# Moving the decay loads of units 8 to 11 from SyncE's DMA queue to GpSimd's in a gated linear attention and expert kernel

## The chip, the cores and the metric

The kernel runs on one core of a Trainium2 chip. The metric is the device time of one execution in microseconds (us); each kernel is run several times and the median stands for it. The kernel before took a median of 179.3 us over five runs, from 176.89 to 180.84 us.

## The reference

Two layers follow each other. The first is a gated linear attention with 4 batches, 8 heads, 768 tokens and a head size of 48. The second is a dense layer with a squared ReLU, from 384 features to 2048 and back, over all 3072 tokens.

```
for t in range(S):
    state = alpha[:, :, t, :, None] * state + np.einsum('bhd,bhe->bhde', k[:, :, t], v[:, :, t])
    y[:, :, t] = np.einsum('bhd,bhde->bhe', q[:, :, t], state)
...
h = x @ w_in
r = np.maximum(h, 0.0)
g = r * r
return (g @ w_out).astype(np.float32)
```

`alpha` is the decay: a number between 0.8 and 1 for every token, head and feature.

## The kernel before, in words

**Units.** The 3072 tokens are cut into 12 units of 256 tokens. Unit g is one block of one batch; units 0 to 3 are the first blocks of the four batches, 4 to 7 the second, 8 to 11 the last. For each unit four inputs are loaded (`load`, line 508): the decays `a`, then `k`, `q` and `v`, 384 KB each, as runs of 384 bytes, into one of four `RAW` buffers.

**Stages of a unit.** The front (`front`, `decays_by_pair`) multiplies the decays of a pair of tokens (`prd`, VectorE, line 615), takes logarithms (`lab` and `la`, ScalarE, lines 618 and 657), sums them along the tokens with a matmul (line 624), takes exponentials (`ek`, `eq`), and multiplies `k` and `q` by them (`qks`, lines 691 and 686). From unit 3 on, two DMA transposes on SyncE's queue turn the result (`kqt`, line 702). Scores follow on TensorE (line 880), a mask on VectorE (`pm`, line 891), the output and the state (lines 772, 783, 751), a copy out of PSUM (`xbf`, line 911) and, for units 4 to 10, one more DMA transpose on SyncE's queue (`xt`, line 932). The dense layer (`moe`) then works through the 2048 hidden features: the first product (line 983) into two PSUM banks in turn, a ReLU that empties each bank (`rr`, ScalarE line 991 or VectorE line 993), a square (`gt`, lines 1001 and 1005), the second product (line 1019), a copy (`osb`) and a store on SyncE's queue (line 1029). The dense work of one unit lies between the attention work of the next.

**What sets the order.** Every instruction is handed to a planner (`Program.add`) with an estimated cost, a priority and the instructions that it depends on. `Program.schedule` plays the program through with these estimates and writes down a fixed order for each engine; some instructions may go to one of two engines, and the planner picks. On the chip every engine runs its list strictly in that order and waits at the head of it, with semaphores placed by `Program.place`. So an estimate that changes can change the order on every engine. For DMAs the planner uses the issue cost (600 ns on SyncE, 930 on GpSimd), a delay to the first byte (`DMA_FIRST`), the transfer time alone (`lag`), and, where several queues have work, shares in proportion to the numbers of `PACKET`, found by the first prefix that matches the operation's name.

**Who gates the loads.** From unit 4 on each load of unit g waits until `q` of unit g-1 has landed (`AFTER`), and from unit 5 on also for a step of unit g-1 (`BEHIND`): its logarithm for `a`, its product for `k`, its first transpose for `q` and `v`. SyncE's queue carries all loads but those of unit 2, which go with the weights through GpSimd's queue, and it carries all transposes and stores as well.

Of the kernel before, what the change touches and what calls it, by code (L numbers as in the profile page):

```python
# [33 lines left out]
class Program:  # L34
# [3 lines left out]
    HOP = 35  # L38
    PE_LATENCY = 170
    DMA_FIRST = {"sp": 1300, "act": 1300, "pool": 2000}  # L40
    PACKET = (("win", 172), ("wout", 490), ("ld", 22), ("tr", 18), ("xt", 18), ("out", 65))
    SBUF_ONLY = ("pr", "bk", "aq", "ekm", "eqm", "sq", "sb", "sd")
    BIAS = {"pool": 300}
    DMA_LAST = 800
# [13 lines left out]
    def add(self, eng, fn, cost, prio, reads=(), writes=(), name="", dma=None, lag=0, after=(), mode=("F", "F"),  # L58
            alts=None):

        reads, writes = ([h for k in keys for h in ((k + (0,), k + (1,)) if len(k) == self.HALVED.get(k[0]) else (k,))]
                         for keys in (reads, writes))
        choices = {eng: (fn, cost)}
        if alts:
            choices.update(alts)
        op = Op(choices, prio, name)
        op.idx = len(self.ops)
        op.lag = lag
        op.mode = mode
        if dma is not None:  # L70
            if dma not in self.dma_sems:
                self.dma_sems[dma] = self.nc.alloc_semaphore("d_" + dma)
                self.dma_count[dma] = 0
            self.dma_count[dma] += 1
            op.sem = (dma, self.dma_count[dma])
        for o in after:
            op.deps[o] = True
        for k in reads:
            w = self.writer.get(k)
            if w is not None:  # L80
                op.deps[w] = True
            if k[0] == "ps":
                for r in self.readers.get(k, ()):
                    op.deps.setdefault(r, False)
        for k in writes:
            w = self.writer.get(k)
            if w is not None:
                op.deps[w] = True
            for r in self.readers.get(k, ()):
                if r is not op:  # L90
                    op.deps.setdefault(r, False)
        for k in reads:
            self.readers.setdefault(k, []).append(op)
        for k in writes:
            self.writer[k] = op
            self.readers[k] = []
        op.deps.pop(op, None)
        self.ops.append(op)
        return op

    def schedule(self):
# [18 lines left out]
        def rates():  # L120
            took = {r: next(t for n, t in self.PACKET if q[0].name.startswith(n)) for r, q in rings.items() if q}
            return {r: t / sum(took.values()) for r, t in took.items()}
# [200 lines left out]
def pe_ns(count, cols, at_once=1):  # L323
    return count * max(cols / 2.4 + 2.5, 25) / at_once
# [6 lines left out]
def dve_ns(n, rate=1.0):  # L331
    return 150 + n / 0.96 / rate
# [6 lines left out]
def bass_gla_recurrent__then__act_relu_squared_kernel(  # L339
# [18 lines left out]
    G = B * NST  # L358
# [4 lines left out]
    ATTN = {1: 13665, 2: 25972, 3: 40856, 4: 50288}  # L363
    DENSE = {0: 21894, 1: 33515, 2: 47958, 3: 58770, 11: 158500}
    POOL_LOADS = {2: "akqv"}
    RATIO = 4
    NRAW, NQKS, NKQT, NPM, NV, NXT, NGT, NRR, NOSB = 4, 3, 3, 2, 4, 4, 2, 4, 4
    WS = 2
# [48 lines left out]
    add = pr.add  # L417
# [17 lines left out]
    for i in range(2):  # L435
        add("dve", fill(LAF[i][:, :, :, D:64].rearrange("p j h d -> p (j h) d"), 0.0), 250, -1e6 - 10,
            writes=[("laf", i)])
        add("dve", fill(LAB[i][:, :, D:64], 0.0), 150, -1e6 + 20, writes=[("lab", i)])
    for i in range(NQKS):
        add("dve", fill(QKS[i][:, :, :, :, D:64].rearrange("p a j h d -> p (a j h) d"), 0.0), 500, -1e6 + 10,  # L440
            writes=[("qks", i, 0), ("qks", i, 1)])
# [7 lines left out]
    for part in (OWN[0:64, 0:H:2], OWN[64:128, 1:H:2]):  # L449
# [3 lines left out]
        writes=[("ident",)])  # L453
# [29 lines left out]
    load_op = {}  # L483
# [4 lines left out]
    def named(x):  # L488
        return next(o for o in pr.ops if o.name == x)

    BEHIND = {"a": "ln", "k": "ekm", "q": "tr0_", "v": "tr0_"}

    def load(g):
        b, i = units[g]
        t0 = i * T
        p0 = g * P
        r, la, qs, kt, pm, vb, x2 = (g % n for n in (NRAW, 2, NQKS, NKQT, NPM, NV, 2))
        first, last = i == 0, i == NST - 1
        sr, sw = 2 * b + i % 2, 2 * b + (i + 1) % 2

        for j, t, nm in ((0, alpha, "a"), (1, k, "k"), (2, q, "q"), (3, v, "v")):
            src = t[b, :, t0:t0 + T, :].rearrange("h (p j) d -> p h (j d)", j=2)
            dst, key = RAW[r][:, j], ("raw", r, j)
            ring, cost, gate = "sp", 600, AFTER.get((g, nm), AFTER.get(g))
            if nm in POOL_LOADS.get(g, ""):
                ring, cost = "pool", 930
            dst = dst.rearrange("p h j d -> p h (j d)")
            load_op[g, nm] = add(ring, lambda e, dst=dst, src=src: e.dma_start(dst, src), cost, (L_PRIO[g] + j if ring == "sp" else W_PRIO[2] + 10 * g + j),  # L508
                writes=[key], name=f"ld{nm}{g}", dma=f"{nm}{r}{ring}", lag=1230,
                after=([load_op[gate]] if gate else []) + ([named(f"{BEHIND[nm]}{g - 1}")] if g >= 5 else []))  # L510

    def front_by_heads(g, p0):

# [96 lines left out]
    def decays_by_pair(g, p0, r, la, last):  # L610
# [11 lines left out]
        def m1(incl):  # L622
            def run(pe):
                ins = pe.matmul(psW[:, 0:HD], (LINC if incl else LSTR)[:], LAB[la][:, :, 0:D])  # L624
                if incl and not last:
                    for p in range(NPR):
                        ins = pe.matmul(psW[:, HD + 2 * p:HD + 2 * p + 2],  # L627
                                        LAB[la][:, 2 * p:2 * p + 2, :].rearrange("p h d -> p (h d)"), ONES2[:],
                                        start=(p == 0), stop=True, skip_group_check=True)
                return ins  # L630
            return run
# [7 lines left out]
        if not last:  # L639
# [5 lines left out]
                          dve_ns(HD))})  # L645
        if g < RATIO:
            add("pe", m1(False), pe_ns(1, HD), p0 + 530, reads=[("lab", la), ("lstr",)], writes=[("ps", "W")],
# [384 lines left out]
    L_PRIO = {g: (g - 4) * P for g in range(G)}  # L1032
    L_PRIO[0], L_PRIO[1] = -9e5, -8e5
    W_PRIO = (-5e5, -4e5, -4.5e5)
    ORDER = ["f0", "k0", "p0", "f1", "y0", "p1", "k1", "y1", "f2", "p2", "k2"]
    for g in range(3, G):
# [3 lines left out]
             ("wout", 1): (2, "k"), 3: ("wout", 0)}  # L1040
    AFTER.update({g: (g - 1, "q") for g in range(4, G)})
    load(0)
    load(1)
    for w in range(WS):
        weight(0, w)
    load(2)
    for w in range(WS):
        weight(1, w)
    for st in ORDER:
        kind, g = st[0], int(st[1:])  # L1050
# [44 lines left out]
```

## Time and profile before

| | us |
|---|---|
| median of five runs | 179.3 |
| the profiled execution, its own time | 178.37 |
| span of that execution | 176.6 |
| TensorE busy in the span | 168.3 |
| VectorE / ScalarE busy | 120.0 / 120.1 |
| GpSimd busy | 15.2 |

The span is the time from the first to the last instruction that the profiler saw. The granted TensorE clock was 1.000. TensorE is busy in 95% of the span, and GpSimd in 9%, nearly all of it in the first 40 us. Of the DMA queues, SyncE's (q1) moved 28.12 MB in 73968 packets and GpSimd's (q0) 4.72 MB in 1536 packets.

From the trace come the times of the loads of the decays. An issue is where the queue's instruction starts; the landing is counted from it.

| unit | decay load issued at, us | us to landing |
|---|---|---|
| 7 | 72.64 | 4.6 |
| 8 | 86.99 | 3.3 |
| 9 | 99.12 | 3.4 |
| 10 | 111.24 | 3.6 |
| 11 | 124.53 | 4.3 |

### The profile page before, as it was taken

What the parts mean: (1) busy time and instruction counts of PE and PEld (TensorE: products, weight loads), DVE (VectorE), ACT (ScalarE), POOL (GpSimd) and SP (SyncE); (2) the same over time, 40 slices, a digit from 0 to 9 for tenths busy, and PEclk for the clock granted to TensorE, in tenths of its full rate; (3) what the DMA queues carried; (4) which work ended last, traced back from release to release, by engine and by line L of the source; (5) the groups of instructions that cost most, each with busy time, mean ns of one, the idle gap of its engine ahead of it and who ended that gap; (6) DMA issues with size and microseconds to landing.
All of it is one profiled execution on the core that took longest, in us unless ns stands there. A gap on an engine that the chain in (4) does not pass through costs nothing.

```text
span 176.6 us, 5120 instructions
## 1 busy us (share of the span) xinstructions
PE 168.3 (95%) x2241; PEld 130.4 (74%) x2241; DVE 120.0 (68%) x198; ACT 120.1 (68%) x215; POOL 15.2 (9%) x24
## 2 busy tenths in 40 slices
PE   7999898999999999999999999996999999999994
PEld 2566797856778777877878788794788697698773
DVE  5597959696949898749589678777759727352230
ACT  4762779677877699659399578496578564475541
POOL 3250740020010003100000000000000000000000
DMA  5999999999999798998599899999797691110112
GB/s 144 324 294 198 279 282 205 231 254 287 214 217 192 199 232 140 261 250 165 157 290 148 229 211 229 253 198 219 196 176 192 150 184 36 45 45 4 45 45 89
DMA packets 75526, 33.16 MB, mean 188 GB/s; under 512 B 70896, under 2 KB 74096, under 8 KB 75504
## 3 DMA queue, kind: packets, MB, share of 16 engines
q1 hardware_dynamic: 73968, 28.12, 69.6%
q0 software_dynamic: 1536, 4.72, 12.1%
q8 instruction: 17, 0.28, 0.6%
q14 instruction: 5, 0.04, 0.1%
HBM read 25.17 MB, written 4.72 MB: 169 GB/s over the span
## 4 chain that ended last, share of the span: by engine, by line
PE 70%; DMA 20%; DVE 3%; SPq 2%; ACT 2%; issue 1%; POOL 1%
PE psWH L983 31%; PE psO L1019 27%; DMA win<-in_moe_w_in_dram 7%; DMA raw<-in_alpha_dram 5%; DMA kqt<-qks 3%; DMA xt<-xbf 3%; DMA raw<-in_q_dram 2%; PE psX L783 2%; SPq L508 2%; PE psX L880 2%; PE psZ L751 2%; PE psX L953 2%; PE psX L772 1%; PE psZ L880 1%; PE psWH L624 1%
## 5 line engine op out<-in xcount | busy, mean ns | idle before, releaser
L983 PE MATMUL psWH<-xt,win 128*128 128x256 bf16 x576 | 74.0, 275 | 3.1 <-DMA xt<-xbf 1.5
L983 PEld LDWEIGHTS psWH<-xt,win 128*128 128x128 bf16 x576 | 64.8, 145 | 8.0 <-DMA xt<-xbf 2.1
L1019 PE MATMUL psO<-wout,gt 128*128 128x384 bf16 x368 | 68.9, 326 | 0.1
L991 ACT ACTIVATE rr<-psWH 128x512 bf16<-128x512 f32 x82 | 48.0, 595 | 22.9 <-PE psWH L983 21.4
L1019 PEld LDWEIGHTS psO<-wout,gt 128*128 128x128 bf16 x368 | 35.1, 98 | 18.3 <-ACT osb L1026 0.3
L1001 DVE TENSOR_TENSOR gt<-rr 128x1024 bf16<-128x1024 bf16 (+1 forms) x40 | 24.0, 602 | 20.4 <-ACT rr L991 20.1
L891 DVE TENSOR_TENSOR pm<-psX,caus 128x1024 bf16<-128x1024 f32 x12 | 14.6, 1218 | 3.9 <-PE psZ L880 3.9
L1005 ACT ACTIVATE gt<-rr 128x512 bf16<-128x512 bf16 (+1 forms) x20 | 16.4, 821 | 0.5
L891 DVE TENSOR_TENSOR pm<-psZ,caus 128x1024 bf16<-128x1024 f32 x12 | 14.6, 1216 | 0.8 <-PE psZ L880 0.8
L686 DVE TENSOR_TENSOR qks<-raw,eq 128x384 bf16<-128x384 f32 x18 | 9.3, 554 | 8.6 <-DMA raw<-in_q_dram 7.0
L1026 ACT ACTIVATE osb<-psO 128x384 f32<-128x384 f32 x19 | 9.3, 492 | 6.3 <-PE psO L1019 5.7
L682 ACT ACTIVATE vbf<-raw 128x768 bf16<-128x768 f32 x10 | 8.4, 842 | 6.8 <-DMA raw<-in_v_dram 6.6
L1063 PE MATMUL psO<-zero 128*128 128x512 bf16 (+1 forms) x35 | 9.7, 412 | 1.3 <-DVE zero L429 1.3
L911 ACT ACTIVATE xbf<-psX 128x768 bf16<-128x768 f32 x11 | 8.9, 805 | 3.0 <-PE psX L772 1.9
L691 DVE TENSOR_TENSOR qks<-raw,ek 128x768 bf16<-128x768 f32 x11 | 10.4, 949 | 0.0
L993 DVE TENSOR_SCALAR rr<-psWH 128x512 bf16<-128x512 f32 x14 | 9.6, 687 | 0.9 <-PE psWH L983 0.3
L657 ACT ACTIVATE la<-raw 128x384 f32<-128x384 f32 x8 | 4.2, 522 | 5.9 <-DMA raw<-in_alpha_dram 5.9
L1063 PEld LDWEIGHTS psO<-zero 128*128 128x128 bf16 x35 | 3.4, 108 | 4.9 <-issue 1.9
L615 DVE TENSOR_TENSOR prd<-raw 128x384 f32<-128x384 f32 x7 | 3.9, 559 | 4.1 <-DMA raw<-in_alpha_dram 4.1
L644 DVE TENSOR_TENSOR ek<-ek,raw 128x384 f32<-128x384 f32 x10 | 5.5, 555 | 1.1 <-ACT ek L635 1.1
L635 ACT ACTIVATE ek<-psWH 128x384 f32<-128x384 f32 x10 | 4.9, 495 | 1.4 <-PE psWH L627 1.4
L751 PE MATMUL psZ<-vbf,qks 64*128 64x96 bf16 x144 | 5.6, 202 | 0.0
(114 smaller groups left out, 159.3 us busy)
## 6 DMA issues: line engine op xcount, KB each, us to landing
out_dram<-osb SPq DMA_DIRECT2D x23, 192.0 KB, 3.1
raw<-in_alpha_dram SPq DMA_DIRECT2D x11, 384.0 KB, 4.3
raw<-in_k_dram SPq DMA_DIRECT2D x11, 384.0 KB, 4.6
raw<-in_q_dram SPq DMA_DIRECT2D x11, 384.0 KB, 4.5
raw<-in_v_dram SPq DMA_DIRECT2D x11, 384.0 KB, 4.9
win<-in_moe_w_in_dram POOLq DMA_DIRECT2D x2, 768.0 KB, 10.0
wout<-in_moe_w_out_dram POOLq DMA_DIRECT2D x2, 768.0 KB, 8.9
raw<-in_alpha_dram POOLq DMA_DIRECT2D x1, 384.0 KB, 5.8
```

Of the source, the lines that this page charges most:

```text
L686: add("dve", lambda e, j=j, dst=dst: e.tensor_tensor(dst, RAW[r][:, 2, :, j, :].rearrange("p (n x) d -> p n x d", x=2), EQ[la][:, j].rearr ...
L691: add("dve", lambda e, a=a, E=E: e.tensor_tensor(QKS[qs][:, a, :, :, 0:D], RAW[r][:, 1 + a].rearrange("p h j d -> p j h d"), E[la][:].rear ...
L751: ins = pe.matmul(banks[c][:, p * 96:p * 96 + 96], QKS[qs][h0:h0 + 64, 0, j, 2 * p:2 * p + 2, :].rearrange("p h d -> p (h d)"), VBF[vb][h0 ...
L891: add("dve", lambda e, hf=hf, psT=psT: e.tensor_tensor(PM[pm][:, hf].rearrange("p r n j t -> p (r n) (j t)"), psT[:, :, :].rearrange("p r ...
L983: ins = pe.matmul(psH[hb][:, i * T:(i + 1) * T], WIN[:, kk, hidden(fj)], mov, start=(kk == 0), stop=(kk == KT - 1))
L991: add("act", lambda e, hb=hb, rr=rr: e.activation(rr, psH[hb], AF.Relu), act_ns(512), pu + 600, reads=[("ps", "H", hb)], writes=[("rr", rb ...
L993: alts={"dve": (lambda e, hb=hb, rr=rr: e.tensor_scalar(rr, psH[hb], 0.0, None, ALU.max), dve_ns(512))})
L1001: add("dve", lambda e, dst=dst, sq=sq: e.tensor_tensor(dst, sq, sq, ALU.mult), 148 + k * 267, pu + 1200, reads=[("rr", rb, h) for h in ran ...
L1005: "act": (lambda e, dst=dst, sq=sq: e.activation(dst, sq, AF.Square), act_ns(k * 512))})
L1019: ins = pe.matmul(psS, GT[gt][:, fj, j, :], WOUT[:, fj, :], start=(fj == 0), stop=(fj == FT - 1))
L1026: add("act", lambda e, ob=ob, psS=psS: e.activation(OSB[ob][:], psS, AF.Copy), act_ns(DM), ps_ + 700, reads=[keyS], writes=[("osb", ob)], ...
L1063: pr.fill(lambda n: lambda pe: pe.matmul(psO[:, 0:n], ZERO[:, 0:128], ZERO[:, 0:n], skip_group_check=True), ((512, 216, 420), (256, 109, 2 ...
```

## The change

The decay loads of units 8, 9, 10 and 11 are issued by GpSimd instead of SyncE. The gates stay as they are, and the other loads stay on their queues. In the planner, GpSimd's loads get names that begin with `ldp`, and with that a number of their own in `PACKET`; their transfer time becomes 1080 ns instead of 1230; this holds for the four loads of unit 2 as well, which went through GpSimd's queue before. For units 8 to 11 the planner's priority is that of the other loads of the unit. The semaphores' names lose the queue's name and gain a `p`.

```diff
-    PACKET = (("win", 172), ("wout", 490), ("ld", 22), ("tr", 18), ("xt", 18), ("out", 65))
+    PACKET = (("win", 172), ("wout", 490), ("ldp", 175), ("ld", 22), ("tr", 18), ("xt", 18), ("out", 65))
...
     POOL_LOADS = {2: "akqv"}
+    POOL_FROM, POOL_WHICH = 8, "a"
+    POOL_LOADS.update({g: POOL_WHICH for g in range(POOL_FROM, G)})
...
             if nm in POOL_LOADS.get(g, ""):
                 ring, cost = "pool", 930
+                nm = "p" + nm
             dst = dst.rearrange("p h j d -> p h (j d)")
-            load_op[g, nm] = add(ring, lambda e, dst=dst, src=src: e.dma_start(dst, src), cost, (L_PRIO[g] + j if ring == "sp" else W_PRIO[2] + 10 * g + j),
-                writes=[key], name=f"ld{nm}{g}", dma=f"{nm}{r}{ring}", lag=1230,
-                after=([load_op[gate]] if gate else []) + ([named(f"{BEHIND[nm]}{g - 1}")] if g >= 5 else []))
+            load_op[g, nm[-1]] = add(ring, lambda e, dst=dst, src=src: e.dma_start(dst, src), cost, (L_PRIO[g] + j if ring == "sp" else W_PRIO[2] + 10 * g + j if g < 3 else L_PRIO[g] + j),
+                writes=[key], name=f"ld{nm}{g}", dma=f"{nm}{r}", lag=1080 if ring == "pool" else 1230,
+                after=([load_op[gate]] if gate else []) + ([named(f"{BEHIND[nm[-1]]}{g - 1}")] if g >= 5 else []))
```

## The prediction

> **What bounds the kernel now.** I began with the page's busy table and groups, then cut the span into stretches of one unit, from one output on TensorE to the next, around the four moved loads:
>
> ```profile
> 89.70:102.20 12.50, 12.50 (x181) 9.82 (x183) 10.28 (x17) 9.38 (x18) 0.00 (x0) 1.00 1.00 223
> 102.20:114.70 12.50, 12.50 (x176) 10.03 (x176) 9.95 (x16) 9.23 (x16) 0.00 (x0) 1.00 0.98 226
> 114.70:128.90 14.20, 12.71 (x175) 9.93 (x176) 9.70 (x16) 9.33 (x17) 0.00 (x0) 1.00 0.91 212
> 128.90:141.40 12.50, 12.50 (x175) 10.02 (x177) 9.69 (x15) 9.43 (x16) 0.00 (x0) 1.00 0.88 164
> ```
>
> The columns are length, then busy us (and instructions) of TensorE, its weight loads, VectorE, ScalarE and GpSimd, then clock, share of DMA time and GB/s. TensorE is busy in 12.50 of 12.50 us. GpSimd does nothing, and the DMA engines are occupied nearly all the time. Only the third stretch has a hole. The chain of waits shows it:
>
> ```profile
> 118.02 0.69 PE psWH L983 x7
> 118.71 4.70 DMA xt<-xbf
> 123.46 0.88 PE psWH L983 x6
> ```
>
> The first dense product waited for its transposed input; the same transpose landed in 2.7 to 2.9 us in the six other units. TensorE lost about 1.5 us here, the largest loss in this half. So the end is set by TensorE, and the moved loads matter only where they make it wait.
>
> Do they? ScalarE's timeline around the load of unit 8:
>
> ```profile
> 88.77 1.07 ACT L991 ACTIVATE rr<-psWH 128x512 bf16<-128x512 f32 x2
> 90.27 0.52 ACT L657 ACTIVATE la<-raw 128x384 f32<-128x384 f32 x1 [0.43 <-DMA raw<-in_alpha_dram]
> 90.70 0.48 ACT L1026 ACTIVATE osb<-psO 128x384 f32<-128x384 f32 x1
> 91.07 0.51 ACT L618 ACTIVATE lab<-prd 128x384 bf16<-128x384 f32 x1
> 91.48 0.80 ACT L911 ACTIVATE xbf<-psX 128x768 bf16<-128x768 f32 x1
> 92.17 1.08 ACT L991 ACTIVATE rr<-psWH 128x512 bf16<-128x512 f32 x2
> ```
>
> The logarithm stands at the head of ScalarE until the decays land, and behind it queue the output copy, a second logarithm and two ReLUs. TensorE's next first product starts at 92.82 with a wait for one of these ReLUs. In all, between 84 and 140 us ScalarE waits 4.2 us for decays, once per unit. The decays are therefore already the last thing to arrive at ScalarE, though TensorE hides most of it.
>
> The loads were not held up on SyncE's queue. Between 84 and 140 us this queue waits 12.6 us, in four waits, for `q` of the unit before, and issues the decays at once when it lands: `q` of unit 7 was issued at 81.72 and took 5.2, which makes 86.92, and the decays follow at 86.99. The change keeps that gate, so no decay load can start sooner.
>
> **What the skill says.** The page "DMA: Bandwidth & Descriptors" bears on it in three places. "Latency and other measured facts" puts the first byte at some 600 ns for SyncE's queue and 1 us for GpSimd's; the trace shows the issue itself at 0.37 us for SyncE's decay loads and 0.95 for GpSimd's one. "SWDGE vs HWDGE vs iDMA" says that the queues feed different rings of one DMA engine, served in turn by packet, and that GpSimd's packets gather up to 4096 bytes. The trace agrees on sizes: 4.72 MB in 1536 packets is 3.07 KB each, 28.12 MB in 73968 is 380 bytes, a ratio of 8. "Issuing engines are not separate DMA queues" says that spreading loads saves only issue time; no run yet shows it. On starved descriptors the page "SBUF — State Buffer", "SBUF: two separate sides", warns of VectorE blocking GpSimd; the trace has GpSimd's four load issues at 0.95 and 0.89 us beside a VectorE busy for 9.04 of 10 us, so I price that at nothing, at most another issue of 0.9.
>
> **The price of the moved load.** Removed from SyncE: four issues of 0.37 us and four transfers. Added to GpSimd: four waits and four issues of 0.95 us. GpSimd's last work was at 73.88 us, so nothing queues behind the wait; if the new order put arithmetic there, the waiting time would fall on whoever needs it.
>
> Its latency without a queue ahead is not shown. GpSimd's loads of unit 2 stood in line behind weights: 5.8 us for the decays. Their landings come out at 23.3, 24.5, 25.6 and 26.5, so one load's data takes 1.07 us. The first weight piece, issued at 9.31, landed 7.9 later, at 17.2; the second at 22.27, 5.07 after it. Taking these 5.07 as the data of one piece leaves 2.8 us for everything else. My estimate for a decay load is 2.8 + 1.07 = 3.9 us from issue. GpSimd also reacts later: 17.2 to 17.53 and 22.27 to 22.55, about 0.28 us, against 0.07 on SyncE. So from the gate 4.2 us, against 3.4, 3.5, 3.7 and 4.4 before (the landing times plus 0.07). Later by 0.8, 0.7, 0.5 and -0.2 us for units 8 to 11. The bounds: every load as fast as SyncE's, since its larger packets take turns against small ones, hence 0; and the 5.8 of unit 2, hence 5.8 + 0.28 - 3.4 = 2.7 later.
>
> What of it reaches TensorE, with the order unchanged? In unit 8 the ReLU is already waited for, so there is no slack. In unit 9 the first ReLU behind the logarithms ends at about 104.8 and TensorE's next first product starts at 105.22: 0.4. In units 10 and 11 it is 117.2 to 117.70 and 131.4 to 131.90: 0.5 each. Stalls: 0.8, 0.3, 0 and 0, **1.1 us together**. The later work of the front is covered: `qks` for `q` at 99.2 us waits for `q`, not for the decays.
>
> **Relief on SyncE.** The second transpose of a unit is held up while loads drain: the first issues took 2.88, 3.37 and 2.86 us in units 8 to 10 (at 100.26, 112.38 and 125.97) against 1.24 for the quickest. One load less ahead frees up to 1.1 us (one load's data), and the stores and `xt` behind it move up. The `xt` issued at 93.92 lands at 96.7, and TensorE needs it at 96.78, so that is worth something when it is late: at most the hole of 1.5 us. I take 0, since one late landing in seven may be chance. The saved data time, 1.23 (the code's own estimate) less 1.07, is 0.16 us a load, and TensorE covers it.
>
> **The order.** The names and `lag` of unit 2's loads change in the planner, four times 150 ns, and GpSimd's transfers there now take 175 shares beside 22 and 18 of SyncE's. Priorities and due times stay. So the order can move on all engines from about 23 us on, although unit 2's transfers themselves are unchanged. Nothing in the trace prices this. From below: the early idle of TensorE between 20 and 60 us, 1.33 + 0.14 + 0.43 + 0.36 = 2.3 us by its busy times, could shrink, say by 1.5. From above: an extra 0.5 us in each of six or seven units, 3. I take +0.9 because `xt`, the ReLUs and `kqt` arrive within a few tenths of their use, and TensorE has nothing spare to win.
>
> **Sum.** 178.37, the profiled execution's own time, + 1.1 + 0 + 0.9 = 180.4. This execution is 0.9 below the median of 179.3, so the forecast for the median is **181.3 us**, 1.1% above.
>
> **Rivals.** (1) *The late decays decide; slower.* If the landing is later by L in each unit, stalls sum to 4L - 1.4 (slacks 0, 0.4, 0.5, 0.5). With L = 1.5, inside my bounds, that is 4.6, and with 0.9 for the order 178.37 + 0.93 + 5.5 = 184.8. From L of about 1.0 on, the loss passes 2%. For it: two engines wait at their heads for the decays already, and 3 KB packets may hold up transposes beside them. Against: the planner itself expects GpSimd's load later and may put other work first. (2) *The relief decides.* `xt` is never late, the hole of 1.5 closes, decays land as before: 179.3 - 1.5 = 177.8; with a luckier early order down to 175.5. Against: decays would have to be no later, and TensorE's 168.3 busy us stay. (3) *The change doesn't do what it says:* loads move at no cost and only the new order shows, anywhere from -1.5 to +3, about 180.2.
>
> **Chances.** The forecast 0.44, rival 1 0.36, rival 2 0.14, rival 3 0.06. Runs of this kernel spread over 2.2%, so about 2% (3.6 us) is what a measurement can tell from no change. Slower than 182.9: all of rival 1, 0.06 of the forecast and 0.02 of rival 3, 0.44. Faster than 175.7: 0.05 of rival 2 and 0.03 of rival 3, 0.08. Between: 0.48. Both ends of the order's price and a lateness up to 1.8 us give a range of 177.5 to 187.0; the forecast's own is 179.5 to 183.2.
>
> **What would show it.** Right: decay issues on GpSimd near 0.95 us, landing 3.7 to 4.4 later; about 0.3 us from gate to issue; ScalarE's waits for decays in units 8 to 11 above 4.2 us, or the logarithms placed behind other work; unit stretches of 12.5 to 13.3 us. Wrong: landings above 5 us or long waits for ReLUs on TensorE (rival 1); second transposes unblocked and no wait for `xt` (rival 2); differences before 84 us that outweigh those after (the order was mispriced). It would also be wrong if GpSimd had been given arithmetic behind its waits.

## The result, and the profile after

The changed kernel took a median of 178.85 us over 36 runs (176.19 to 181.72), the kernel before 178.22 us over 71 runs (175.48 to 180.95). The ratio is 1.0051, with a 95% interval from 1.0029 to 1.0073: slower by about 0.9 us, where the forecast had been 2.0 us slower. The medians are of all executions, while ratios and intervals, here and below, compare only those within 1.5% of a kernel's fastest. The spread of single runs, 5.5 us, is six times the difference, so the reasons have to be read from places in the trace and not from the total alone.

The profiled execution of the changed kernel took 181.72 us, the longest of its runs, and its TensorE clock fell to 0.90 for one stretch; three further profiles of the same kernel (below) therefore stand beside it. In the changed kernel the lines move: the decay load is line 511, the first dense product 986, the ReLUs 994 (ScalarE) and 996 (VectorE).

From the page of the changed kernel, its DMA queues and two groups of instructions:

```profile
q1 hardware_dynamic: 69808, 26.55, 66.5%
q0 software_dynamic: 1984, 6.29, 15.1%
...
L511 POOL DMA_DIRECT2D raw<-in_alpha_dram x5 | 4.6, 912 | 53.4 <-DMA raw<-in_q_dram 36.1
...
L684 POOL CAST vbf<-raw 128x768 bf16<-128x768 f32 x7 | 6.1, 871 | 29.6 <-DMA raw<-in_v_dram 29.5
```

Four loads of 384 KB have gone from the first queue to the second, in 448 packets more there and 4160 fewer here, and each issue costs GpSimd 0.91 us on average, as predicted. What the prediction had only mentioned as a risk is in the last line: GpSimd now makes seven casts of `v`, one before. The planner gave it those of units 8 to 11, right behind the loads, and those of units 2 and 4. GpSimd's timeline in the changed kernel:

```profile
85.43 0.96 POOL L511 DMA_DIRECT2D raw<-in_alpha_dram  x1 [10.99 <-DMA raw<-in_q_dram]
98.79 0.89 POOL L511 DMA_DIRECT2D raw<-in_alpha_dram  x1 [12.40 <-ACT rr L994]
99.74 0.83 POOL L684 CAST vbf<-raw 128x768 bf16<-128x768 f32 x1
112.80 0.88 POOL L511 DMA_DIRECT2D raw<-in_alpha_dram  x1 [12.23 <-DMA raw<-in_q_dram]
```

The loads of units 8 to 11 landed 5.7, 7.4, 4.8 and 6.0 us after issue; before it had been 3.3, 3.4, 3.6 and 4.3. What the 7.4 did is in VectorE's, ScalarE's and TensorE's timeline of the changed kernel:

```profile
106.22 0.52 ACT L660 ACTIVATE la<-raw 128x384 f32<-128x384 f32 x1 [3.21 <-DMA raw<-in_alpha_dram]
106.22 0.56 DVE L618 TENSOR_TENSOR prd<-raw 128x384 f32<-128x384 f32 x1 [5.47 <-DMA raw<-in_alpha_dram]
106.65 0.79 ACT L914 ACTIVATE xbf<-psX 128x768 bf16<-128x768 f32 x1
106.70 0.55 DVE L849 TENSOR_TENSOR smd<-psZ,sbd 128x384 bf16<-128x384 f32 x1
107.17 0.68 DVE L996 TENSOR_SCALAR rr<-psWH 128x512 bf16<-128x512 f32 x1
...
107.90 1.50 PE L986 MATMUL psWH<-xt,win 128*128 128x256 bf16 x6 [2.26 <-DVE rr L996]
```

Both engines stand at the head of their lists until the decays come, VectorE for 5.47 us. The ReLU that would empty TensorE's PSUM bank is third in VectorE's list, so TensorE waits 2.26 us for a ReLU whose own input had been ready all along. This is the predicted kind of stall, larger than predicted. The wait of 1.5 us for `xt` of the kernel before is absent: in none of the four profiles of the changed kernel does TensorE wait for `xt` more than 0.12 us. Late transposes are not gone, though. The `xt` issued between 130 and 135 us lands 3.8 to 4.6 us after issue in all four, just in time for TensorE.

### The profile page after: what moved, and what is told of

Read it like the earlier page. It is cut to its first block, busy times and chain, and to the rows that moved or that the text cites. A ratio compares the mean times of both kernels' runs of the same rounds, so it can differ in the third digit from the quotient of the medians.

```text
span 180.0 us, 5139 instructions
## 1 busy us (share of the span) xinstructions
PE 171.1 (95%) x2241; PEld 131.4 (73%) x2241; DVE 115.0 (64%) x188; ACT 121.6 (68%) x219; POOL 24.2 (13%) x34
## 4 chain that ended last, share of the span: by engine, by line
PE 44%; DMA 33%; ACT 8%; SPq 6%; DVE 5%; issue 2%; POOL 1%; DVEq 0%
PE psWH L986 19%; PE psO L1022 17%; DMA raw<-in_alpha_dram 16%; DMA raw<-in_q_dram 9%; DMA win<-in_moe_w_in_dram 4%; ACT rr L994 3%; DMA raw<-in_v_dram 3%; SPq L705 2%; SPq L511 2%; PE psX L956 1%; SPq L1032 1%; DVE pm L894 1%; ACT eq L640 1%; DVE rr L996 1%; ACT ek L638 1%
## 5 line engine op out<-in xcount | busy, mean ns | idle before, releaser
L986 PE MATMUL psWH<-xt,win 128*128 128x256 bf16 x576 | 75.5, 278 | 3.4 <-DVE rr L996 2.6
L994 ACT ACTIVATE rr<-psWH 128x512 bf16<-128x512 f32 x88 | 51.8, 595 | 23.5 <-PE psWH L986 22.1
L1004 DVE TENSOR_TENSOR gt<-rr 128x1024 bf16<-128x1024 bf16 (+1 forms) x39 | 23.3, 601 | 23.3 <-ACT rr L994 23.0
L1008 ACT ACTIVATE gt<-rr 128x512 bf16<-128x512 bf16 (+1 forms) x21 | 17.5, 833 | 0.5
L1029 ACT ACTIVATE osb<-psO 128x384 f32<-128x384 f32 x22 | 10.8, 492 | 10.2 <-PE psO L1022 9.6
L511 POOL DMA_DIRECT2D raw<-in_alpha_dram x5 | 4.6, 912 | 53.4 <-DMA raw<-in_q_dram 36.1
L694 DVE TENSOR_TENSOR qks<-raw,ek 128x768 bf16<-128x768 f32 x11 | 11.4, 1034 | 0.0
L684 POOL CAST vbf<-raw 128x768 bf16<-128x768 f32 x7 | 6.1, 871 | 29.6 <-DMA raw<-in_v_dram 29.5
L849 DVE TENSOR_TENSOR smd<-psZ,sbd 128x384 bf16<-128x384 f32 x8 | 4.4, 552 | 4.8 <-PE psX L775 4.8
L996 DVE TENSOR_SCALAR rr<-psWH 128x512 bf16<-128x512 f32 x8 | 5.5, 688 | 0.7 <-PE psWH L986 0.5
```

Source lines behind the costliest of these rows:

```text
L511: load_op[g, nm[-1]] = add(ring, lambda e, dst=dst, src=src: e.dma_start(dst, src), cost, (L_PRIO[g] + j if ring == "sp" else W_PRIO[2] + ...
L694: add("dve", lambda e, a=a, E=E: e.tensor_tensor(QKS[qs][:, a, :, :, 0:D], RAW[r][:, 1 + a].rearrange("p h j d -> p j h d"), E[la][:].rear ...
L986: ins = pe.matmul(psH[hb][:, i * T:(i + 1) * T], WIN[:, kk, hidden(fj)], mov, start=(kk == 0), stop=(kk == KT - 1))
L994: add("act", lambda e, hb=hb, rr=rr: e.activation(rr, psH[hb], AF.Relu), act_ns(512), pu + 600, reads=[("ps", "H", hb)], writes=[("rr", rb ...
L1004: add("dve", lambda e, dst=dst, sq=sq: e.tensor_tensor(dst, sq, sq, ALU.mult), 148 + k * 267, pu + 1200, reads=[("rr", rb, h) for h in ran ...
L1008: "act": (lambda e, dst=dst, sq=sq: e.activation(dst, sq, AF.Square), act_ns(k * 512))})
```

## The experiments

All ratios are to the kernel before, timed in the same session, each with its 95% interval. Several kernels use a helper that runs after the planner and moves an instruction from one engine's finished list to another's, with a semaphore of its own if it is a DMA, so that nothing else in the order changes. The old order is that of the kernel before, the new order that of the changed kernel. The helper:

```
def shift(op, to, ahead=None):
    pr.order[op.eng].remove(op)
    op.eng = to
    ...
    queue = pr.order[to]
    queue.insert(queue.index(ahead) if ahead else sum(o.start <= op.start for o in queue), op)
    ...
```

I use three measures from the traces, each a mean over units 8 to 11. The gate is the landing of `q` of the unit before; "from the gate" is the time until the decays have landed; "gate ahead" is how long before TensorE's next first dense product the gate lands (a wait of TensorE itself lengthens it). "Four stretches" is the time on TensorE from the state product of unit 7 to that of unit 11; four full stretches without a wait take 4 x 12.48 = 49.9 us, the floor (12.53 a stretch in the new order).

| kernel | decays on, order | from the gate, us | gate ahead, us | four stretches, us | ratio |
|---|---|---|---|---|---|
| before | SyncE, old | 3.7 | 4.4 | 51.7 | 1 |
| sp_new_order | SyncE, new | 3.5 | 4.3 | 52.2 | 1.0027 |
| prices_only | SyncE, old but for unit 2's prices | 3.9 | 4.5 | 52.1 | 0.9983 |
| pool_old_order | GpSimd, old | 5.1 | 5.5 | 50.4 | 0.9979 |
| old_order_again | GpSimd, old | 5.4 | 5.6 | 51.2 | 0.9955 |
| after | GpSimd, new | 6.3 | 5.8 | 55.2 | 1.0051 |
| after_again | GpSimd, new | 5.8 | 5.5 | 51.9 | 0.9963 |
| after_third | GpSimd, new | 5.4 | 5.6 | 53.9 | 1.0072 |
| after_fourth | GpSimd, new | 5.6 | 5.3 | 51.4 | 1.0005 |
| store_later | GpSimd, new, one store moved | 5.1 | 5.7 | 50.4 | 1.0003 |

### The changed kernel again, and its two halves

**after_again**, **after_third** and **after_fourth** are the changed kernel unaltered.

> The changed kernel once more, for a second profile, since the profiled execution shown with the result took 181.7 us, near the slow end of its own 36 runs (176.2 to 181.7). All theories: a ratio of 1.003 to 1.008 to the kernel before. Late-decays theory: GpSimd's four decay loads land 4.5 us or more after issue (5.7, 7.4, 4.8 and 6.0 in the first profile), well above the 3.9 that was estimated, and ScalarE waits for decays for more than 4.2 us. Chance theory: the 7.4 does not come back, and the four landings are near 4.

> The changed kernel a third time, since the recorded ratio of 1.0051 and the 0.9963 of the second measurement exclude each other. Slower theory: 1.003 to 1.007. Equal theory (the difference between sessions is larger than the intervals): 0.995 to 1.003. In the profile: decay landings of 4.7 us or more from issue, and gates 5.0 us or more ahead of the dense product, as in the first two.

> The changed kernel as the frame for casts_back and store_later in the same session. Order theory: 1.002 to 1.008, GpSimd's decay loads land 5.2 us or more after issue on average. Session theory (it equals pool_old_order, and only sessions differ): 0.995 to 1.001.

Measured: 0.9963 (0.9917 to 1.0009), 1.0072 (1.0038 to 1.0105), 1.0005 (0.9966 to 1.0044). The first two exclude each other, so sessions differ by as much as the effect. With the first measurement the four ratios average 1.0023, and two of the four intervals contain 1: that the change loses half a per cent isn't firm. By the readings set out before it, after_fourth speaks for a difference between sessions. The late landings are constant: 4.6 to 7.4 us in all sixteen loads, mean 5.5. In the fourth profile the stretches, in the columns of the prediction, are:

```profile
89.40:101.94 12.54, 12.54 (x192) 9.98 (x183) 8.96 (x14) 10.31 (x19) 1.72 (x2) 1.00 0.95 212
101.94:114.46 12.52, 12.52 (x182) 9.96 (x174) 8.60 (x13) 9.63 (x18) 1.80 (x2) 1.00 0.98 216
114.46:127.18 12.72, 12.72 (x184) 9.90 (x175) 8.51 (x13) 9.53 (x18) 1.71 (x2) 1.00 0.89 206
127.18:140.76 13.58, 12.79 (x183) 9.89 (x175) 8.60 (x13) 9.53 (x18) 0.83 (x1) 1.00 1.06 169
```

Here only the last unit pays, 1.1 us, after a landing of 6.0.

**pool_old_order**: the kernel before, with only the four loads moved from list to list.

```diff
     pr.schedule()
+    for g in range(8, G):
+        shift(load_op[g, "a"], "pool")
```

> The order of every engine is that of the kernel before; only the four decay loads of units 8 to 11 are taken out of SyncE's list and put into GpSimd's. This measures the late decays with the order unchanged. Prediction's step (stalls of 1.1 us): ratio 1.006. Theory A (late decays cost more, and the new order gives it back): stalls of 2 to 5 us, ratio 1.011 to 1.028. Theory B (late decays cost little): ratio 0.998 to 1.004.

> pool_old_order once more (order before, decays of units 8 to 11 on GpSimd), beside another set of runs of the kernel before. If the order is what costs the changed kernel its 0.5 to 0.7%: ratio 0.994 to 1.002, no wait for xt, decay landings of 4.5 to 5.3 us. If late decays cost it: 1.003 to 1.010, with waits for ReLUs or logarithms of more than 1 us in units 8 to 11.

Measured: 0.9979 (0.9944 to 1.0014), and 0.9955 (0.9922 to 0.9989) in another session. The stretches of pool_old_order:

```profile
91.47:104.47 13.00, 12.80 (x190) 9.86 (x182) 10.36 (x17) 9.42 (x18) 0.89 (x1) 1.00 0.90 205
104.47:116.95 12.48, 12.48 (x183) 10.00 (x174) 9.50 (x15) 9.07 (x16) 0.88 (x1) 1.00 1.01 211
116.95:129.43 12.48, 12.48 (x183) 10.00 (x174) 9.76 (x16) 9.13 (x17) 0.88 (x1) 1.00 0.92 225
129.43:141.91 12.48, 12.48 (x183) 10.00 (x174) 9.51 (x15) 9.48 (x17) 0.00 (x0) 1.00 0.72 157
```

Three stretches are at the floor of 12.48 although the decays come 1.5 us later from the gate than before. The hole of the third stretch is gone. And the gate lies 5.5 us ahead of TensorE instead of 4.4, which pays for most of GpSimd's latency. A queue of SyncE that is shorter by a load, and so brings `q` in earlier, is one explanation; ballast and k_on_pool below test it. It can't be the whole: for unit 8 the gate is 5.5 us ahead instead of 3.7, and there `q` landed before the first moved load was due. Theory A, that the late decays cost more and the new order gives it back, falls, and the prediction's step of 1.006 lies outside both intervals: with the old order the move costs nothing or gains a little. In the session in which both ran, the changed kernel (0.9963) was no slower than this one (0.9979).

**sp_new_order**: the reverse, the changed kernel's order with the four loads back on SyncE, ahead of `k`.

```diff
     pr.schedule()
+    for g in range(8, G):
+        shift(load_op[g, "a"], "sp", load_op[g, "k"])
```

> The order of every engine is that of the changed kernel, with the four value casts of units 8 to 11 on GpSimd, but the four decay loads are issued by SyncE again, each ahead of its unit's k load. This measures the new order alone. Prediction's step (order +0.9 us): ratio 1.005. Theory A: the new order is free or gains, ratio 0.990 to 1.001. Theory B, in which the new order makes up the loss: ratio 1.003 to 1.008.

Measured: 1.0027 (0.9993 to 1.0061), which bounds the new order by itself between nothing and 1.1 us and doesn't decide between the expectations. Its chain of waits has the hole again:

```profile
120.19 0.71 PE psWH L986 x7
120.89 4.63 DMA xt<-xbf
125.52 0.14 issue
125.66 0.85 PE psWH L986 x6
```

**prices_only** has the planner's new prices but no load of units 8 to 11 on GpSimd.

```diff
-    POOL_FROM, POOL_WHICH = 8, "a"
+    POOL_FROM, POOL_WHICH = 12, "a"
```

> The planner has the new prices and names, but no load of units 8 to 11 goes to GpSimd; only the loads of unit 2 are planned otherwise, so the order differs through the early part and what follows from it. If the early order carries the loss: ratio 1.003 to 1.008. Theory A and the view that the loss sits in units 8 to 11: ratio 0.997 to 1.003.

Measured: 0.9983 (0.9953 to 1.0013). The early order carries no loss. The wait for `xt` is there as well, 1.6 us. So with all the loads of these units on SyncE three of three profiles have this wait, at 1.5 to 1.6 us and in the same unit; with the decays on GpSimd none of the two of the old order and none of the four of the changed kernel has it. So it goes with the queue that issues the decays, in either order, and is not chance.

### What the latency is worth

**late_more** adds a fill of 2048 columns of an unused buffer between the gate and each load, in the old order.

```diff
+    idle = nc.alloc_sbuf_tensor("idle", [128, 4, 2048], BF16)
+    for g in range(8, G):
+        op = load_op[g, "a"]
+        shift(op, "pool")
+        op.fn = lambda e, go=op.fn, g=g: (e.memset(idle[:, g - 8], 0.0), go(e))[-1]
```

> As pool_old_order, but GpSimd fills 2048 bf16 columns of an unused buffer after the gate and before each of the four loads, so that the decays land 1 to 2 us later still, call it M. Prediction's sum (each unit pays its own stall): with the landings of pool_old_order about 0.4 us ahead of TensorE's dense product and M = 2, some 1.2 us in each of four units, 5 us, ratio 1.025 to 1.03. Once theory (a stall moves TensorE back against the gate, so that the next unit has that much more slack): 1 to 2.5 us in all, ratio 1.004 to 1.012, and the distance from the gate to the dense product grows by the first stall and stays.

Measured: 1.0401 (1.0302 to 1.0500), from three executions. The issue came 1.5 us later after the gate, and with landings of 7.2, 4.2, 7.1 and 5.5 us from issue the decays came 2.7 us later in the mean. The waits of TensorE from 77 us on:

```profile
PE psWH L624 <- ACT lab L618: 8.2, 3, 5.1
PE psWH L983 <- ACT rr L991: 0.4, 2, 0.2
```

The stretches were 20.05, 12.48, 15.11 and 14.16 us; in the first the granted clock was 0.83. So the slack was nearly used up in pool_old_order, and a further 2.7 us costs some 7 by the ratio. The once theory falls: units 8, 10 and 11 paid. But unit 9, after the largest stall, paid nothing: its gate lay 7.7 us ahead, and its load landed quickest. In this trace stalls are neither paid once nor simply four times.

**ballast** keeps SyncE's queue as full as before: it loads the same decays a second time, through SyncE, into a buffer that nothing reads.

```diff
+        shift(load_op[g, "a"], "pool")
+        extra.fn = lambda e, dump=dump, src=src: e.dma_start(dump[:].rearrange("p (h d) -> p h d", h=H), src)
+        extra.deps = {load_op[g - 1, "q"]: True}
+        queue.insert(queue.index(load_op[g, "k"]), extra)
```

> As pool_old_order (the order before, decay loads of units 8 to 11 moved to GpSimd), but SyncE issues a load of the same 384 KB at the old place of each moved load, into a buffer that nothing reads. So SyncE's queue keeps its four issues and transfers while the decays still come late. Relief theory (one load less on SyncE's queue lets q, which is the gate of the next decays, land earlier against TensorE, and that pays for GpSimd's latency): from the gate to TensorE's first dense product after it 3.7 to 5.3 us again, as before, instead of 5.3 to 5.9; TensorE waits for ReLUs behind the decays, ratio 1.005 to 1.015. Rival (the latency never mattered, the slack was simply larger): ratio 0.995 to 1.002, as for pool_old_order, and the gate stays 5.3 or more ahead.

Measured: 1.0199 (1.0135 to 1.0264), with these stretches:

```profile
90.75:103.73 12.98, 12.78 (x191) 9.88 (x182) 10.21 (x16) 9.25 (x17) 0.89 (x1) 1.00 0.88 218
103.73:117.22 13.49, 12.88 (x184) 9.87 (x174) 9.55 (x15) 8.98 (x16) 0.88 (x1) 1.00 1.06 240
117.22:130.91 13.69, 12.88 (x184) 9.87 (x175) 9.55 (x15) 8.97 (x16) 0.88 (x1) 1.00 0.96 224
130.91:143.76 12.85, 12.70 (x183) 9.92 (x174) 9.56 (x15) 9.40 (x17) 0.00 (x0) 1.00 0.90 172
```

With the extra load the move costs 2%, and every unit pays, more than the 1.005 to 1.015 expected. But one expectation of the relief theory failed: the gate is 5.7 us ahead, not 3.7 to 5.3; TensorE's waits, 1.7 us in all four stretches, can add some 0.4 us a unit to that distance and don't bring it back to 4.4. Nor did the wait for `xt` return, although SyncE's queue carried as many loads as before: in the third stretch `xt` landed 1.5 us ahead of its use. The loss comes with decays that took 5.9 us from issue, a microsecond more than in pool_old_order. The extra load is traffic as well as a place in the queue, and this run doesn't separate the two.

**early_gate** takes the gate away from the moved loads, which then start after the logarithm of the unit before.

```diff
+        shift(load_op[g, "a"], "pool")
+        load_op[g, "a"].deps.pop(load_op[g - 1, "q"])
```

> As pool_old_order, but the four decay loads no longer wait for q of the unit before, only for its logarithm (and their buffer), so they start some 8 us earlier and land long before use. TensorE-bound theory: nothing waits for decays in units 9 to 11, but the time hardly moves, ratio 0.992 to 1.000. Rival (late decays are a real cost in pool_old_order): clearly below it, 0.985 to 0.992. Rival (larger packets beside transposes hurt): q, v or xt land later and the ratio is 1.003 or more.

Measured: 1.0079 (1.0041 to 1.0116), in the session of after_third. The decays landed 7 us or more ahead of use, TensorE waited for neither ReLUs nor logarithms in units 8 to 11, and still the time was not better. Latency is therefore not all that counts. The signs of the third reading came true: `q` took 4.6 to 5.0 us to land against 3.8 to 4.2 in pool_old_order, and the two `xt` issued between 105 and 120 us took 4.9 and 4.8 us against 3.0 and 2.8. Whether larger packets or only more traffic at that time did it isn't settled. Its stretches were 12.85, 12.95, 12.71 and 12.48 us, a small loss in three units instead of one hole; together they are 0.7 us shorter than before, so this profile doesn't show where the time of 1.0079 went.

### Why GpSimd's loads land late

**hold_transposes** lets the two transposes wait until the decays have landed (old order).

```diff
+        shift(load_op[g, "a"], "pool")
+        for c in range(2):
+            named(f"tr{c}_{g - 1}").deps[load_op[g, "a"]] = True
```

> As pool_old_order (decays of units 8 to 11 on GpSimd, order before), but the two transposes of the unit before wait until these decays have landed, so nothing of SyncE's queue but k and stores runs beside the decay load. If the transposes beside it are what makes GpSimd's landing long (5.7, 7.4 and 7.2 us where transposes were issued within 1.2 us of it, 4.2 to 4.8 where they came later): all four landings 3.7 to 4.4 us. If GpSimd's latency is its own: 4.5 to 5.5 as in pool_old_order. The transposes themselves come 3 to 4 us later and with them q and the gate, so the time is no measure of the change; 1.01 to 1.04.

Measured: landings of 5.1, 4.5, 4.5 and 5.1 us; ratio 1.0425 (1.0336 to 1.0514), from two executions. Without transposes beside it the load still takes 4.8 us, as in pool_old_order (4.8). So the transposes don't make the ordinary landing long. What does, within GpSimd's path or in the loads and stores that still run beside it, this run doesn't say.

**casts_back** and **store_later** ask what lengthens it from 5.0 in the old order to 5.5 in the new.

```diff
+    for g in range(8, G):
+        shift(named(f"vc{g}"), "act")
```

> The changed kernel with the value casts of units 8 to 11 given back to ScalarE at their planned times, all else as in the new order. If the casts on GpSimd lengthen the loads or hold something up: faster than after_fourth by 0.003 or more, landings 4.5 to 5.3 us. If they are a gain that relieves ScalarE: slower by 0.002 or more, with more waits of TensorE for ReLUs. If they are beside the point: within 0.002.

```diff
+    queue = pr.order["sp"]
+    for g in range(8, G):
+        at, behind = queue.index(load_op[g, "k"]), queue.index(named(f"tr1_{g - 1}"))
+        for o in [o for o in queue[at:behind] if o.name.startswith("out")]:
+            queue.remove(o)
+            queue.insert(behind, o)
...
```

> The changed kernel with the store that SyncE issues between k and the two transposes moved behind the transposes, in units 8 to 11. If that store beside the decay load makes its landing longer: landings 4.5 to 5.2 us instead of 4.6 to 7.4, fewer waits for ReLUs, faster than after_fourth by 0.003 or more. If not: landings as before and within 0.002.

Measured: casts_back 0.9976 (0.9944 to 1.0007) with landings of 5.2 to 5.8 us; store_later 1.0003 (0.9971 to 1.0036) with landings of 5.4, 4.6, 4.7 and 4.7. The new order issues a store between `k` and the transposes, as SyncE's timeline of after_again shows:

```profile
98.05 0.37 SPq L511 DMA_DIRECT2D raw<-in_k_dram  x1
98.85 0.36 SPq L1032 DMA_DIRECT2D out_dram<-osb  x1
99.25 5.36 SPq L705 DMA_TRANSPOSE kqt<-qks  x2
```

With this store moved, SyncE's timeline of store_later:

```profile
97.25 0.37 SPq L511 DMA_DIRECT2D raw<-in_k_dram  x1
99.98 3.15 SPq L705 DMA_TRANSPOSE kqt<-qks  x2
103.17 1.78 SPq L1032 DMA_DIRECT2D out_dram<-osb  x2
```

Three landings of four came down to 4.6 to 4.7, and the four stretches to 50.4 us. The casts don't matter for the landing. The store beside the load may: in the old order it is there in unit 8 alone, whose landings were the longest there too (5.3 and 5.6). But store_later doesn't show it cleanly. In the three units that improved, the transposes also started later, 1.4 to 2.7 us after the load's issue against 1.0 to 1.4 in after_fourth; in unit 8, where they started 0.9 us after it, the load took 5.4 us without the store. The gain by the stretches, 0.9 us against after_fourth's 51.4, isn't confirmed by the ratios, 1.0003 and 1.0005.

### A load that can bear the latency

**k_on_pool** moves `k` instead of the decays, in the old order, for units 8 to 11; **k_on_pool_5** for units 5 to 11, twice.

```diff
+    for g in range(5, G):
+        shift(load_op[g, "k"], "pool")
```

> The order before on every engine, but instead of the decays the k loads of units 8 to 11 go to GpSimd; the decays stay on SyncE. SyncE's queue is relieved of one load per unit just as in the change, while k, which its product uses 3.3 us after it landed in unit 8, can bear GpSimd's latency. Theory (relief closes the wait for xt of 1.5 to 1.8 us that three of three profiles with all loads on SyncE show in unit 9 to 10, and late decays are what the change pays): no wait for xt above 0.5 us, decays land 3.3 to 4.3 us after issue, ratio 0.988 to 0.996. Rival (the closed hole is chance): ratio 0.998 to 1.004 and the hole is there again. Rival (3 KB packets hold up transposes): ratio above 1.004.

> As k_on_pool, but for the k loads of units 5 to 11. Theory: the hole closes as well, and units 5 to 7 gain little since their stretches carry other waits; ratio 0.985 to 0.996. Rival (GpSimd's waits for q hold up its arithmetic of units 5 to 7, prd, sbd and a cast): above k_on_pool by 0.003 or more.

> k loads of units 5 to 11 on GpSimd, order before, a second time. If its gain is real: 0.990 to 0.997. If it was the session: 0.998 to 1.002.

Measured: 0.9973 (0.9932 to 1.0013) for units 8 to 11; 0.9939 (0.9906 to 0.9972) and 0.9984 (0.9946 to 1.0022) for units 5 to 11. The decays, still on SyncE, land 3.3 to 4.5 us after issue as before. The waits for `xt` are 1.2 us in two waits, 0.8 in two waits, and nothing. In k_on_pool the longer one stands where the hole was:

```profile
123.97 0.88 PE L983 MATMUL psWH<-xt,win 128*128 128x256 bf16 x6 [0.90 <-DMA xt<-xbf]
```

That is above the 0.5 us that the theory allowed, and the gate is 5.0, 4.5 and 4.8 us ahead in the three runs, little more than the 4.3 to 4.5 with all loads on SyncE. So a queue shorter by one load closes the hole only in part, and doesn't by itself move the gate as moving the decays did. By the expectation of its repetition, 0.9984 is the session and no gain. The two runs of units 5 to 11 average 0.9962, the two of the decays in the old order 0.9967: no version stands out.

## Why the prediction was right or wrong

The side was right in the first measurement and the size was not: 1.1% was forecast, 0.51% measured, and 0.2% in the mean of four measurements. Two terms of the sum were mis-sized with opposite signs, and a third was not found.

- **"Relief on SyncE ... I take 0, since one late landing in seven may be chance."** This is the step that failed. The late `xt` was no chance: TensorE's wait for it stands in every profile with all the loads of units 8 to 11 on SyncE and in none of the changed kernel. The term is -1.5 us, the bound that the prediction named and didn't use. With the hole closed, the gate lies 1.1 us further ahead of TensorE (5.5 us instead of 4.4 in the old order), which the prediction did not see: it held that no decay load can start sooner. That the relief of SyncE's queue does this is not shown. A full queue in ballast brought back neither the wait nor the old gate, and relief by `k` left 0.9 us of the wait. What is shown is that both go with the decays' move; the mechanism stays open.
- **The landing, "2.8 + 1.07 = 3.9 us from issue".** Measured: 5.5 in the mean of the changed kernel's sixteen loads, 4.8 to 5.1 in the old order. The 2.8 came from a first weight piece and a difference of two landings, with other traffic beside both. GpSimd's reaction to the gate was right, 0.29 us. So the decays were later by 2.1 us (5.8 from the gate less 3.7), not by 0.45.
- **"Stalls: ... 1.1 us together."** The four stretches of the changed kernel lose 5.2, 1.9, 4.0 and 1.4 us against the floor, 3.1 in the mean; the first and the third each hold a stretch at a granted clock of 0.90. By rival 1's sum, a lateness of 2.1 would have cost 4 x 2.1 - 1.4 = 7.0; with the gate 1.1 us ahead it is 4 x 1.0 - 1.4 = 2.6. That the earlier gate makes up this difference is worked out, not measured by itself.
- **The order, +0.9 us.** Not found as such: prices_only 0.9983, sp_new_order 1.0027 with an interval that reaches both 0 and 0.9 us. It put a store beside the load; whether that matters is not shown.
- **Casts on GpSimd** were named as what would make the prediction wrong; they came, and casts_back at 0.9976 shows no more than their small price, if any.

Put together, the changed kernel loses 3.1 us in the four stretches, in the mean of its four profiles, and the kernels with decays on SyncE lose 2.1 (1.8, 2.3 and 2.2, of which the hole is 1.5). The difference of 1.0 is close to the 0.9 us measured, but that agreement is luck. It rests on the profiled executions of 181.7 and 180.6 us, in each of which TensorE waited for a ReLU (2.3 and 1.9 us) and the clock fell to 0.90 in that stretch (the last number but two), shown for after, then for after_third:

```profile
102.94:119.54 16.60, 14.34 (x183) 10.72 (x174) 9.19 (x14) 9.57 (x19) 1.71 (x2) 0.90 0.96 185
90.19:106.51 16.32, 14.43 (x191) 10.57 (x183) 9.79 (x16) 10.30 (x20) 1.72 (x2) 0.90 0.99 225
```

Those of 178.5 and 177.3 us lose 1.9 and 1.4, about the 1.8 of the kernel before at 178.4. So the runs show where the change loses and where it gains; they don't derive the 0.9 us. Rival 1 had the place of the loss and rival 2 the place of the gain; each was right about its half.

What stays open: why the hole closes and the gate moves when the decays go to GpSimd, why GpSimd's landing reached 7.4 us once (7.1 and 7.2 in late_more), and where early_gate lost its time. The difference between sessions, up to 1.1% for one and the same kernel, has no explanation here either.

## What to carry to other kernels

A load that moves to another queue changes two queues: it takes on the latency of the new one, and what stood behind it in the old one may come earlier. Price both before saying that either is nothing, and look whether a transfer on the old queue is itself the gate of the moved one. Put the load back as a dummy before calling the shorter queue the cause; here that test did not bear it out. And treat a wait that stands in a trace at one place as real until a second profile lacks it.

## What the runs showed of the hardware

- A 384 KB load issued by GpSimd lands 4.8 to 5.1 us after issue where the same load by SyncE takes 3.5 to 3.9, although its landings in a row come no slower (1.1 us apart for GpSimd's four loads of unit 2, 1.2 for SyncE's first eight loads of the kernel before). The difference is there without transposes beside it (hold_transposes, 4.8).
- GpSimd starts the issue 0.29 us after the landing of `q` that it waits for, SyncE 0.02 us.
- The landing of GpSimd's load varies with what runs beside it: 5.9 us in the mean with a second 384 KB load on SyncE's queue (ballast), 4.8 and 5.1 in the same order without it.
